# A chain of attention and two mixture-of-experts layers: the descriptor scratch of the software DMA queue at 1024 bytes per partition

## The chip, the cores and the metric

One Trainium2 chip, one core. The metric is the device time of one execution in microseconds (us), as the median of several runs. The engines are TensorE (PE), VectorE (DVE), ScalarE (ACT), GpSimd (POOL) and SyncE (SP). DMAs that SP or ACT issue go through a hardware queue; DMAs that POOL issues go through the software queue, which is the one that the change touches.

## The reference

Three layers in a row, on 4 batches of 576 tokens with 8 heads of 64 (2304 rows of 512).

```python
scores = q @ k.T / 8;  cum = cumsum(max(s, 0))
scores = where(causal, -1e9, scores + min(cum_j - cum_i, 0))
x = softmax(scores) @ v                           # rows of 8*64 = 512
# first mixture: 8 experts, each takes at most 288 rows, best logits first
logits = x @ w_gate;  assigned = greedy(order of all logits, cap = 288)
out[mask_e] = relu(x[mask_e] @ w1[e]) @ w2[e]
# second mixture, of out: only rows with x @ w_skip > 0
e = argmax(xc @ w_gate2);  p = softmax(xc @ w_gate2)[e]
y[mask_e] = xc + p * (relu(xc @ v1[e]) @ v2[e])   # other rows keep x
```

## The kernel before

Attention runs head by head in a hand-written order of steps. Heads come in 16 groups of two; for 15 of them POOL loads keys and queries a second time with a DMA that rounds them to the matmul's 32-bit form (`load_a`, L88; the first of these groups as two half loads, so 16 such DMAs). The rows of attention's output and the logits go to a scratch tensor `xs` in HBM through SP.

The first mixture routes expert by expert: VectorE and TensorE find the 288 rows of an expert by counting, and put their numbers in `tok`. For each expert, POOL gathers the rows in three indirect DMAs of 96 (`gather`, L993), TensorE multiplies them through both weight matrices, and POOL scatters the three results to `out` (`outp`, L1093). For the last expert the gathered rows are first scattered once as they are (`claim`, L1105), so that their places are taken. Each scatter is followed by a memset of one element, the spacer.

The second mixture sorts the rows that are computed into lists of 128 for each expert (`tab`, `tk`), with the number of lists in `nt`. It gathers 128 rows with an indirect DMA (`gather2`, L1241), skips list places that hold no row, multiplies, and scatters the results (`ffn2`, L1333; `ffn2s` for up to 64 rows, L1395). The order of instructions within an expert comes from a planner (`Plan`) with estimated durations; each engine then runs its own queue in that order, held by semaphores.

After the first list of an expert, a register that holds the number of its lists decides whether more is to be done:

```python
        rn = nc.values_load(nt[0:1, e:e + 1], min_val=0, max_val=NJ)      # L1510
        ...
            with tc.If(rn == 2):                                          # L1516
                ffn2s(e, i2, col(tk, e, 1), tabp[:, 1, e, 1:2])
            ...
            with tc.If(rn > 2):                                           # L1520
                ffn2(e, i2, 2, col(tk, e, 1), tabp[:, 1, e, 1:2])
...
    with tc.If(rm > 3):                                                   # L1560
```

L1560 is the case of an expert with more than three lists, behind the last expert. Every engine loads the number and branches for itself. Each branch holds a scatter; where it is skipped, POOL runs an INC_SWDGE_SEM in its place, so that the software queue's semaphores stand as if the scatter had run. The kernel ends (L1622) with SP reading all semaphores, a DRAIN on each engine and a barrier.

[...]

## Time and profile before

| | |
|---|---|
| median of 3 runs | 731.12 us (728.97 to 734.17) |
| profiled execution | 729.32 us; span from the first to the last instruction 727.5 us |
| granted TensorE clock, mean | 0.967 |
| TensorE busy | 660.5 us, 91% of the span |
| VectorE, ScalarE, GpSimd busy | 73%, 55%, 37% |
| software queue (q0) | 7008 packets, 24.25 MB, 12.6% of the DMA engines' time |
| hardware queue of SP (q1) | 28272 packets, 94.87 MB, 41.3% |

Times within the profile count from the first instruction. "Busy" leaves out the queues' own instructions: branches, register loads, semaphores, drains and the issuing of DMAs. The view of one source line lists them too, with an engine's name followed by q.

### The profile page before, as it was taken

Reading aid. Unit: us, or ns where it says so; the run is one execution under the profiler, and the core shown is the slowest. Engines: PE = TensorE matmul, PEld = TensorE weight load, DVE = VectorE, ACT = ScalarE, POOL = GpSimd, SP = SyncE. Lnnn points to the kernel's source line nnn. Section 1 sums busy time; section 2 is a strip of 40 time slices with the busy share of each in tenths; the row PEclk is TensorE's granted clock in tenths of the full one; section 3 lists DMA queues with packets and bytes.
Section 4 is the critical chain, followed back from the end, with each engine's and each line's share of the span. In section 5 each row is a group of like instructions: output and inputs, shape, how many; then the busy total and the mean of one; then the engine's idle time right before and its main releaser. Section 6 shows DMA issues by size and latency. Waiting matters only on the chain. (4 is left out here: it accounts for less than half of the span.)

```text
span 727.5 us, 14103 instructions
## 1 busy us (share of the span) xinstructions
PE 660.5 (91%) x4666; PEld 575.3 (79%) x4667; DVE 531.1 (73%) x1604; ACT 403.3 (55%) x910; POOL 269.3 (37%) x379
## 2 busy tenths in 40 slices
PE   4689999999996489999999999999999999999990
PEld 4578989989895368888988898999987878777770
DVE  7568888798886687888989898644486195884640
ACT  8758888888883132442524334443372274884540
POOL 4799769968720410302212232430204032321200
PEclk9989999999998589999999999999999999999996
DMA  7867897897612343562716346740395076695400
GB/s 161 186 160 184 193 233 163 204 207 170 173 37 74 116 153 116 175 243 60 279 55 247 139 164 240 247 148 1 108 405 208 14 272 246 243 332 207 133 9 14
DMA packets 35939, 122.25 MB, mean 168 GB/s; under 512 B 6480, under 2 KB 6480, under 8 KB 34064
## 3 DMA queue, kind: packets, MB, share of 16 engines
q1 hardware_dynamic: 28272, 94.87, 41.3%
q0 software_dynamic: 7008, 24.25, 12.6%
q10 hardware_dynamic: 576, 2.10, 0.9%
q8 instruction: 43, 0.70, 0.4%
q14 instruction: 40, 0.33, 0.1%
HBM read 101.12 MB, written 13.76 MB: 158 GB/s over the span
## 5 line engine op out<-in xcount | busy, mean ns | idle before, releaser
L987 DVE TENSOR_TENSOR wl<-raw,wh 128x1024 fp32r<-128x1024 f32 x112 | 134.3, 1216 | 22.7 <-ACT wh L985 21.5
L985 ACT CAST wh<-raw 128x1024 fp32r<-128x1024 f32 x112 | 115.0, 1048 | 36.2 <-DMA raw<-in_w_dram 23.7
L256 ACT ACTIVATE z<-z,sums 128x576 f32<-128x576 f32 (+2 forms) x144 | 84.7, 589 | 3.4 <-DVE sums L248 1.7
L248 DVE CUSTOM_DVE_ANT_0 z<-s,mask 128x576 f32<-128x576 f32 (+2 forms) x144 | 70.3, 513 | 14.5 <-PE s L237 14.0
L272 PE MATMUL pt<-ident,z 128*128 128x128 f32 (+1 forms) x464 | 77.4, 282 | 1.6 <-DVE ptl L291 1.2
L236 PE MATMUL s<-kq 128*128 128x288 f32 (+2 forms) x192 | 63.7, 343 | 11.8 <-ACT kq L114 8.8
L291 DVE TENSOR_TENSOR ptl<-pt,pth 128x512 fp32r<-128x512 f32 (+2 forms) x128 | 68.1, 551 | 7.4 <-ACT pth L286 7.1
L993 POOL DMA_INDIRECT xb<-xs,k_tok x24 | 29.6, 1234 | 113.3 <-DVE k_tok L739 34.4
L1049 PE MATMUL y<-hf,rb 128*128 128x288 f32 x256 | 70.5, 411 | 0.0
L1093 POOL DMA_INDIRECT out_dram<-xb,k_tok x24 | 27.0, 1126 | 110.9 <-ACT xb L1076 99.8
L286 ACT CAST pth<-pt 128x512 fp32r<-128x512 f32 (+2 forms) x128 | 59.3, 474 | 12.7 <-PE pt L272 10.0
L237 PE MATMUL s<-ka,qa 128*128 128x288 f32 (+2 forms) x192 | 52.3, 309 | 6.8 <-DMA qa<-kq 3.8
L272 PEld LDWEIGHTS pt<-ident,z 128*128 128x128 f32 (+1 forms) x464 | 52.8, 142 | 6.7 <-issue 2.8
L1051 ACT CAST yr<-y 128x288 fp32r<-128x288 f32 x32 | 12.8, 399 | 72.7 <-PE y L1049 69.4
L1049 PEld LDWEIGHTS y<-hf,rb 128*128 128x128 f32 x256 | 45.5, 189 | 9.0
L300 PE MATMUL y<-pth,vhl 128*128 128x384 f32 (+2 forms) x160 | 50.5, 324 | 0.2 <-ACT yT L317 0.2
L1018 PE MATMUL h<-xth,wh 128*128 128x288 f32 x256 | 48.6, 308 | 1.4 <-DVE r_ac L663 0.9
L236 PEld LDWEIGHTS s<-kq 128*128 128x128 f32 x192 | 37.0, 193 | 15.6 <-issue 13.6
L1018 PE MATMUL h<-xth,wl 128*128 128x288 f32 x256 | 46.6, 299 | 0.0
L1018 PE MATMUL h<-xtl,wh 128*128 128x288 f32 x256 | 46.4, 300 | 0.1
L300 PE MATMUL y<-ptl,vhl 128*128 128x384 f32 (+2 forms) x160 | 46.1, 317 | 0.0
L143 POOL TENSOR_TENSOR qa<-raw,kq 64x576 fp32r<-64x576 f32 x30 | 42.6, 1419 | 5.5 <-DMA kq<-in_kqT_dram 3.6
(343 smaller groups left out, 1729.7 us busy)
## 6 DMA issues: line engine op xcount, KB each, us to landing
raw<-in_v_dram SPq DMA_DIRECT2D x64, 512.0 KB
raw<-in_w_dram SPq DMA_DIRECT2D x46, 512.0 KB
raw<-in_kqT_dram SPq DMA_DIRECT2D x14, 576.0 KB
kq<-in_kqT_dram POOLq DMA_DIRECT2D x14, 576.0 KB, 7.2
rb<-in_w_dram SPq DMA_DIRECT2D x14, 512.0 KB
vraw<-in_vL_dram SPq DMA_DIRECT2D x16, 320.0 KB
xs<-xb SPq DMA_DIRECT2D x16, 288.0 KB
ka<-kq SPq DMA_DIRECT2D x14, 288.0 KB
```

What stands on the lines that cost most here:

```text
L236: nc.tensor.matmul(rows[:, o + c0:o + c1], qs_, kb[:, i, c0:c1], start=True, stop=False)
L237: nc.tensor.matmul(rows[:, o + c0:o + c1], ql_, ka[:, i, c0:c1], start=False, stop=True)
L248: nc.vector.tensor_tensor_reduce(z[:, :w], ps[:, o:o + w], mk, op0=OP.add, op1=OP.min, scale=-0.125, scalar=3e38, accum_out=sums[h // 2][: ...
L256: nc.scalar.activation(z[:, :w], z[:, :w], AF.Exp, bias=sm[:, 0:1], scale=-1.0, accum_out=sm[:, 1:2])
L272: nc.tensor.transpose(ps[:jw, k, :], p[:, I0[jb]:I0[jb] + jw], ident)
L286: nc.scalar.copy(hview(PTB[h % 2][0], ib, jbs), ps[:, :len(jbs), :])
L291: nc.vector.tensor_tensor(hview(PTB[h % 2][1], ib, jbs), ps[:, :len(jbs), :], hview(PTB[h % 2][0], ib, jbs).bitcast(F32), op=OP.subtract)
L300: nc.tensor.matmul(y[:, a2 - 192:S - 192], vhl[:, h % G, jb].rearrange("p a d -> p (a d)"), PTB[h % 2][t][:, jb, a2 - 192:], start=n_ == 0 ...
L985: return nc.scalar.copy(WH[j], RAW[i])
L987: op("DVE", 1.13, f"raw{i} wh{j}a wh{j}b", v, lambda: V.tensor_tensor(WL[j], RAW[i], WH[j].bitcast(F32), op=OP.subtract), pr)
L1018: x = nc.tensor.matmul(ps, a[(p * HC + k) % NP][:, m * 128:(m + 1) * 128], xt[c][:, k, :], start=k == 0 and i == 0, stop=k == 3 and i == 2)
L1049: op("PE", 0.49, f"rb{r} hf{k}", f"yb{b}", lambda r=r, o=o, k=k: nc.tensor.matmul(ps, RB[r][:, o:o + 128], hf[:, k - HS1, :], start=False, ...
```

## The change

The program is built with a descriptor scratch of 1024 bytes per partition. The tiles then begin 15360 bytes lower in each partition; their sizes and order are as before, and so is every instruction on every engine.

```diff
@@ -1612,7 +1612,7 @@
 
     data = dict(**host_layout(q, k, v, s, moe_w_gate),
                 **host_moe(moe_w1, moe_w2, moe2_w_gate, moe2_w_skip, moe2_w1, moe2_w2))
-    nc = bacc.Bacc("TRN2", target_bir_lowering=False, num_devices=1)
+    nc = bacc.Bacc("TRN2", target_bir_lowering=False, num_devices=1, dynamic_dma_scratch_size=1024)
     arrays, args = {}, []
     for name in _INS:
         a = np.ascontiguousarray(data[name])
```

## Rows read from the trace of the kernel before

**Rows 1.** Busy us by stretch; columns: stretch, length, PE, PEld, DVE, ACT, POOL, clock, DMA.

```profile
560.00:711.00 151.00, 144.04 (x703) 116.21 (x702) 93.99 (x105) 86.21 (x117) 31.05 (x48) 1.00 0.51 179
711.00:727.50 16.50, 0.00 (x0) 0.00 (x0) 0.00 (x0) 0.00 (x0) 0.00 (x0) 0.58 0.04 15
```

**Rows 2.** Instructions in order of time, all engines, 708 to 728 us; start, length.

```profile
709.80 0.99 POOL L1333 DMA_INDIRECT out_dram<-xb,tk  x1 [10.54 <-DVEq L1516]
710.77 0.09 POOL L1335 MEMSET spacer<- 1x1 f32 x1
```

**Rows 3.** Single source lines: count, ns min/median/max, first and last start (some in windows).

```profile
L1615 POOLq INC_SWDGE_SEM  x1: 31/31/31, 0.2 to 0.2; - x1
...
L1516 POOLq INC_SWDGE_SEM  x5: 1780/1920/2080, 597.5 to 711.0; - x5
...
L1520 POOLq INC_SWDGE_SEM  x6: 1726/1894/2075, 599.6 to 713.4; - x6
...
L1516 POOLq INC_SWDGE_SEM  x1: 1780/1780/1780, 597.5 to 597.5; - x1
...
L1520 POOLq INC_SWDGE_SEM  x1: 1726/1726/1726, 599.6 to 599.6; - x1
...
L1516 POOLq INC_SWDGE_SEM  x1: 2080/2080/2080, 711.0 to 711.0; - x1
...
L1520 POOLq INC_SWDGE_SEM  x1: 2075/2075/2075, 713.4 to 713.4; - x1
...
L1560 POOLq INC_SWDGE_SEM  x1: 2099/2099/2099, 716.6 to 716.6; - x1
```

**Rows 4.** Single source lines: the kernel's start (L1615) and end (L1622).

```profile
L1615 POOLq DRAIN  x1: 196/196/196, 0.4 to 0.4; - x1
...
L1622 SPq EVENT_SEMAPHORE  x14: 17/28/28, 718.6 to 727.5; - x14
...
L1622 POOLq DRAIN  x3: 46/103/7992, 718.7 to 727.2; - x3
L1622 SPq DRAIN  x3: 7/7/13, 719.4 to 726.9; - x3
```

**Rows 5.** DMA issues of POOL, whole span: count, KB each, median us to landing.

```profile
kq<-in_kqT_dram POOLq DMA_DIRECT2D x14, 576.0 KB, 7.2
...
kq<-in_kqT_dram POOLq DMA_DIRECT2D x2, 288.0 KB, 7.0
...
out_dram<-xb,k_tok POOLq DMA_INDIRECT x27, 4.1
xb<-xs,k_tok POOLq DMA_INDIRECT x24, 3.9
...
xb<-out_dram,tk POOLq DMA_INDIRECT x15, 5.8
out_dram<-xb,tk POOLq DMA_INDIRECT x11, 4.6
...
xb<-out_dram,tks POOLq DMA_INDIRECT x2, 7.1
out_dram<-xb,tks POOLq DMA_INDIRECT x2, 3.8
```

**Rows 6.** DMA issues of POOL, 598 to 728 us.

```profile
xb<-out_dram,tk POOLq DMA_INDIRECT x9, 5.9
out_dram<-xb,tk POOLq DMA_INDIRECT x9, 4.0
```

**Rows 7.** POOL in order of time, 546 to 561 us; five DMAs between these two.

```profile
546.48 0.94 POOL L1093 DMA_INDIRECT out_dram<-xb,k_tok  x1 [0.44 <-ACT xb L1076]
...
559.88 1.03 POOL L1333 DMA_INDIRECT out_dram<-xb,tks  x1 [0.23 <-issue]
```

**Rows 8.** Waits of TensorE: us in total, times, longest.

```profile
PE tr L1004 <- DMA xb<-xs,k_tok: 1.8, 2, 1.5
```

**Rows 9.** DMA issues of POOL, 709 to 728 us.

```profile
out_dram<-xb,tk POOLq DMA_INDIRECT x1, 3.5
```

## The prediction

> **What bounds the kernel now.** I read the busy time by stretch first [rows 1]. From 560 to 711 us TensorE is busy for 144.04 of 151 us: there the matmuls set the pace, and what GpSimd (POOL) does beside them is cover. The last 16.5 us are different in kind: no engine has a busy microsecond in them. The list of instructions in order of time [rows 2] says the same: the last counted instruction is the spacer memset behind the last scatter, which ends at 710.86, and the span ends at 727.5. The chain of waits stops there as well, because it follows counted work only. So the question for this change is what fills 16.6 us in which nothing computes.

> The view of single source lines answers it, since it also lists the queue's own instructions, which are not counted as busy. For each `tc.If` whose branch is skipped, POOL runs one INC_SWDGE_SEM, which books the scatter that the branch would have issued: five on L1516, six on L1520, one on L1560 [rows 3]. The last three start at 711.0, 713.4 and 716.6 and take 2.080, 2.075 and 2.099 us, one behind the other. Then POOL's DRAIN of the kernel's end (L1622) starts at 718.7 and takes 7.992 us [rows 4]. The sum is 6.25 + 7.99 = 14.2 us; loads, branches and the closing barrier are the rest. The program's end waits for POOL's queue alone.

> **The change, part by part.** It adds and moves no instruction; it cuts the room to a sixteenth.

> How many entries n stay listed: if 97 fit in 16384 bytes, at least 97 / 16 = 6 fit in 1024; above that the trace sets no bound but 97. I take 6, the proportion that the rows give, and keep both ends below.

> INC_SWDGE_SEM at the end: 0.30 + 6 x 0.0184 = 0.41 in place of 2.085, three times: 5.03 us less. With the price of the empty queue, 0.031, it would be 6.2.

> DRAIN: 6 x 0.082 = 0.49 us in place of 7.99. What is late next is SyncE, which reads its semaphores from 718.6 and reaches its own drain at 719.4 [rows 4], 0.8 us behind the third INC_SWDGE_SEM. So 8.0 us shrink to 0.8, not to 0.5: 7.2 less. The last scatter doesn't stand in the way: issued at 709.80, it lands 3.5 us later [rows 9], at 713.3, and the new drain would begin at 718.7 - 5.0 = 713.7. That margin is only 0.4 us, so a late landing would be the next bound.

> The nine earlier INC_SWDGE_SEM shrink by about 1.5 us each, 13 us of POOL's queue. I count them at nothing: they lie in 597 to 711, where TensorE is nearly full [rows 1]. If that cover is gone, the gathers behind them only start earlier.

> Taking old entries off is new work, 97 - 6 = 91 times. The nearest row is the DRAIN's 0.082 per entry: 7.5 us over the whole of POOL, which has room. It is on the path of the end where TensorE waits for a gather today, the first three gathers [rows 8], and at the last scatter: 4 x 0.082 = 0.33 us more. Bounds: nothing at all (the entry landed long ago), or 0.30 each, the intercept above: 1.2.

> Waiting for room is the wait that the change may add. Behind a gather that waits stand POOL's next gathers and scatters, and TensorE's transposes wait for the rows. The closest packing that the traced order shows is the DMA at 559.88; with room for six, the one that it must push out was issued at 546.48, 13.4 us earlier [rows 7], and the slowest kind lands in 7.2 [rows 5]. So if the oldest goes first, nobody waits.

> All tiles move 15360 bytes down. No row shows a cost that depends on an address; I take zero.

> Sum: -5.03 - 7.2 + 0.33 = -11.9 us. The profiled execution took 729.32 us with a span of 727.5, so it becomes 717.4. It lies 1.8 under the median of the three runs, 731.12; against that median the forecast is 719.2.

> Each further entry in the list costs 3 x 0.0184, and 0.082 once the drain passes SyncE's 0.8. With 20 entries the gain is 10.3; with 48, half of today's, 6.4. The best case (0.031 for INC_SWDGE_SEM, no cost of taking off) gains 13.4.

> [...]

> **The rivals.**
> *The end's drain is a fixed cost.* If the 7.99 us wait for something other than the list (say, all earlier writes), only the three INC_SWDGE_SEM shrink: -5.03 + 0.33 = -4.7, or 726.4. For it: there is one long DRAIN only, so its slope is not measured, as that of INC_SWDGE_SEM is. Against it: the last DMA landed 5 us before it began, and it fits 97 equal steps. [...]

> *The list isn't bounded by the scratch.* If the bookkeeping lives elsewhere and is only cleared by the last drain, no step changes, and the time is 731.1. For it: nothing in the trace shows an entry being dropped. Against it: a room that is reused has to know which of its users are done.

> *Room is freed by waiting for the newest, not the oldest.* Then POOL stops each time the room is full until all that it holds has landed: 97 / 6 = 16 stops of about 4.9 us (the medians of rows 5 weighted by their counts). It decides from the point at which more than two of them are on TensorE's path, since two cost 9.8 and the end gives back 11.9. With four, 731.1 - 11.9 + 19.6 = 738.8, slower; with eight, 758. For it: gathers come in groups of two to five, and TensorE has waited for one already [rows 8]. [...]

> **How the numbers follow.** Forecast 0.77, fixed drain 0.06, unbounded list 0.10, waiting for the newest 0.07. The likeliest gives 719.2. Its own range: best case 717.7 less 2.2 for the lowest of the runs shown, so 715.5; worst case with 20 entries and 1.2 for taking off, gain 9.4, so 721.7, plus 3 for the highest run. To hold 8 in 10 it has to take in the fixed drain: 715 to 727.5. A measurement of this kernel tells about 1% from no change (the three runs span 0.7%): faster by that means under 723.8, which is the forecast but for its edge, 0.75; within 1% are the fixed drain, the unbounded list and that edge, 0.18; slower is the last rival, 0.07.

> **What would show each step.** POOL's INC_SWDGE_SEM on L1516, L1520 and L1560 near 0.4 us and no longer growing; the long DRAIN on L1622 under 1 us; the stretch behind the last scatter about 5 us in place of 16.6; everything up to 711 us in place within its noise. I am wrong if INC_SWDGE_SEM still grows past 1 us, if the DRAIN stays near 8 while INC_SWDGE_SEM falls, or if POOL's indirect DMAs take several us each or TensorE's waits for gathers exceed the 1.8 us of now [rows 8].

## The result

The change made the kernel faster, by a little over half of what was forecast. The changed kernel's median is 724.83 us (722.98 to 727.07, four runs) against 731.49 us for the kernel before on the same chip; the ratio is 0.9906, with a 95% interval of 0.9881 to 0.9932. That is 6.7 us less, where 11.9 were forecast, and short of the 1% from which the prediction would have called it faster (under 723.8). The interval and the repeats below show that it is no chance. The profiled execution took 724.78 us with a span of 723.1.

The end did what the prediction said. The time ahead of the end did not stay in place: it grew by about 6 us. The experiments are about where these come from.

### The profile page after: what moved, and what is told of

Its sections match the earlier page's. It is cut to its first block, busy times and chain, and to the rows that moved or that the text cites. A ratio compares the mean times of both kernels' runs of the same rounds, so it can differ in the third digit from the quotient of the medians.

```text
span 723.1 us, 14104 instructions
## 1 busy us (share of the span) xinstructions
PE 667.0 (92%) x4667; PEld 581.1 (80%) x4667; DVE 531.7 (74%) x1604; ACT 402.3 (56%) x910; POOL 269.2 (37%) x379
## 5 line engine op out<-in xcount | busy, mean ns | idle before, releaser
L987 DVE TENSOR_TENSOR wl<-raw,wh 128x1024 fp32r<-128x1024 f32 x112 | 134.4, 1216 | 23.0 <-ACT wh L985 19.7
L1018 PE MATMUL h<-xth,wh 128*128 128x288 f32 x256 | 50.5, 318 | 2.0 <-DVE r_ac L663 0.9
L1018 PE MATMUL h<-xtl,wh 128*128 128x288 f32 x256 | 48.4, 309 | 0.1
L1018 PE MATMUL h<-xth,wl 128*128 128x288 f32 x256 | 48.1, 306 | 0.0
L236 PEld LDWEIGHTS s<-kq 128*128 128x128 f32 x192 | 37.0, 193 | 13.4 <-issue 11.1
```

The lines of the kernel that those rows point to most:

```text
L236: nc.tensor.matmul(rows[:, o + c0:o + c1], qs_, kb[:, i, c0:c1], start=True, stop=False)
L987: op("DVE", 1.13, f"raw{i} wh{j}a wh{j}b", v, lambda: V.tensor_tensor(WL[j], RAW[i], WH[j].bitcast(F32), op=OP.subtract), pr)
L1018: x = nc.tensor.matmul(ps, a[(p * HC + k) % NP][:, m * 128:(m + 1) * 128], xt[c][:, k, :], start=k == 0 and i == 0, stop=k == 3 and i == 2)
```

## The profile after

**The end.** Instructions in order of time, all engines, from 716 us; they answer to [rows 2]:

```profile
717.96 0.99 POOL L1333 DMA_INDIRECT out_dram<-xb,tk  x1 [10.55 <-DVEq L1516]
718.94 0.09 POOL L1335 MEMSET spacer<- 1x1 f32 x1
```

Busy us by stretch of the changed kernel, to [rows 1]:

```profile
560.00:719.00 159.00, 152.29 (x739) 122.63 (x737) 99.44 (x123) 86.62 (x118) 36.09 (x56) 1.00 0.49 176
719.00:723.10 4.10, 0.00 (x0) 0.00 (x0) 0.00 (x0) 0.00 (x0) 0.03 (x1) 0.53 0.18 59
```

Single source lines of the changed kernel, to [rows 3, 4]:

```profile
L1516 POOLq INC_SWDGE_SEM  x5: 240/280/340, 605.9 to 719.2; - x5
...
L1520 POOLq INC_SWDGE_SEM  x6: 252/270/286, 606.6 to 719.8; - x6
...
L1560 POOLq INC_SWDGE_SEM  x1: 299/299/299, 721.1 to 721.1; - x1
...
L1622 POOLq DRAIN  x3: 46/103/642, 721.5 to 722.8; - x3
L1622 SPq DRAIN  x3: 7/7/13, 722.2 to 722.5; - x3
```

INC_SWDGE_SEM takes 0.24 to 0.34 us throughout and no longer grows; the long DRAIN is 0.642 us in place of 7.992. Behind the last spacer lie 4.1 us in place of 16.6, so the end gave 12.5 us; the prediction had 12.2.

**The loss.** The last scatter starts at 717.96, not at 709.80 [rows 2]. So 8.2 us of this profile were lost before it. Following instruction by instruction, the changed kernel is 1.4 us ahead of the kernel before when the first list of tokens is ready, and 4.6 us behind when the second expert's first gather starts (296.51 against 291.94; before, then after):

```profile
291.94 1.17 POOL L993 DMA_INDIRECT xb<-xs,k_tok  x1 [34.39 <-DVE k_tok L739]
```

```profile
296.51 1.18 POOL L993 DMA_INDIRECT xb<-xs,k_tok  x1 [38.05 <-DVE k_tok L739]
```

The place is the first expert's start. First the kernel before, GpSimd (POOL) and VectorE (DVE) in order of time:

```profile
252.60 0.16 DVE L739 SCALAR_TENSOR_TENSOR k_tok<-r_iv 96x3 int32<-96x3 f32 x1
...
253.66 1.07 POOL L993 DMA_INDIRECT xb<-xs,k_tok  x1 [8.69 <-DVE r_v L605]
...
253.82 1.22 DVE L987 TENSOR_TENSOR wl<-raw,wh 128x1024 fp32r<-128x1024 f32 x1
...
255.03 0.93 POOL L993 DMA_INDIRECT xb<-xs,k_tok  x1 [0.30 <-issue]
255.41 1.34 DVE L622 TENSOR_TENSOR r_ge<-r_kb,th 128x1134 bf16<-128x1134 f32 x1 [0.38 <-PE y L1410]
...
256.27 1.28 POOL L993 DMA_INDIRECT xb<-xs,k_tok  x1 [0.30 <-issue]
```

Then the same instructions of the changed kernel:

```profile
251.25 0.16 DVE L739 SCALAR_TENSOR_TENSOR k_tok<-r_iv 96x3 int32<-96x3 f32 x1
...
252.46 1.22 DVE L987 TENSOR_TENSOR wl<-raw,wh 128x1024 fp32r<-128x1024 f32 x1
252.53 2.10 POOL L993 DMA_INDIRECT xb<-xs,k_tok  x1 [8.93 <-DVE r_lo L629]
...
254.06 1.34 DVE L622 TENSOR_TENSOR r_ge<-r_kb,th 128x1134 bf16<-128x1134 f32 x1 [0.37 <-PE y L1410]
...
254.93 1.26 POOL L993 DMA_INDIRECT xb<-xs,k_tok  x1 [0.30 <-issue]
255.31 2.35 DVE L987 TENSOR_TENSOR wl<-raw,wh 128x1024 fp32r<-128x1024 f32 x2
...
256.50 1.96 POOL L993 DMA_INDIRECT xb<-xs,k_tok  x1 [0.30 <-issue]
```

Read the order first. Before, the first gather starts 0.90 us after the list of tokens (252.76 to 253.66) and 0.16 us ahead of VectorE's subtraction. After, it starts 1.12 us behind the list (251.41 to 252.53), and the subtraction has begun 0.07 us earlier. Now the ends: the subtraction ends at 253.68 and the gather at 254.63, 0.95 us behind; the comparison on L622 ends at 255.40 and the second gather at 256.19, 0.79 behind; the pair on L987 ends at 257.66 and the third at 258.46, 0.80 behind. Each of these gathers seems to wait for the VectorE instruction that was running when it started, and the third gather of the kernel before does so too (255.41 + 1.34 = 256.75, end at 257.55). From the list to the end of the third gather it was 4.79 us and is 7.05, 2.26 more. (The list of tokens is written on L739; its end is counted.)

What follows on TensorE, in order of time: the last transposes of the first expert and its first matmuls, in the kernel before,

```profile
262.61 0.52 PE L1004 MATMUL tr<-ident,xb 96*128 96x96 f32 x4 [1.53 <-DMA xb<-xs,k_tok]
...
263.70 1.05 PE L1018 MATMUL h<-xth,wh 128*128 128x288 f32 x6 [0.46 <-ACT xth L1008]
```

and in the changed kernel:

```profile
264.46 0.87 PE L1004 MATMUL tr<-ident,xb 96*128 96x96 f32 x4 [2.77 <-DMA xb<-xs,k_tok]
...
265.91 1.81 PE L1018 MATMUL h<-xth,wh 128*128 128x288 f32 x6 [0.45 <-ACT xth L1008]
```

The waits of TensorE say the same, to [rows 8]:

```profile
PE tr L1004 <- DMA xb<-xs,k_tok: 4.7, 3, 2.8
```

The same six matmuls take 1.81 us for 1.05. Busy time and granted clock from 262 to 270 us show why, before and after:

```profile
262.00:270.00 8.00, 6.92 (x63) 6.35 (x64) 6.02 (x15) 3.34 (x6) 0.00 (x0) 1.00 0.36 144
```

```profile
262.00:270.00 8.00, 5.08 (x30) 4.51 (x30) 3.17 (x9) 2.37 (x3) 0.00 (x0) 0.50 0.30 97
```

Behind the longer wait the granted clock stays at 0.50 through this stretch, where it was 1.00. TensorE gets 30 matmuls done instead of 63.

From the list of tokens to the second expert's first gather it is 39.18 us before and 45.10 after. The other profiles place the loss there too: 45.21 and 44.83 us in the next two at 1024 bytes, 37.8 to 40.3 in every profile below in which the first gather came before VectorE's instruction and none waits for room.

## Experiments

Three causes were open: the tiles that moved 15360 bytes down, the small queue itself, and chance in one execution. "Default" is the scratch of the kernel before, 16384 bytes: the 1024 of the change and the 15360 by which it moved the tiles. In the table, "ahead" is the median less what the profile has behind the start of the last scatter; for the kernel before it is 712.0 to 712.6 in the first three comparisons and 710.5 in the last. "Lead" is how long the first gather starts ahead of VectorE's large instruction (below zero: behind its start); that is the subtraction on L987, and in the run with POOL held back more the comparison on L622.

| kernel | lead, us | first three gathers, us | clock 262 to 270 | last scatter | median us | ahead | ratio to before |
|---|---|---|---|---|---|---|---|
| before | +0.16 | 1.07, 0.93, 1.28 | 1.00 | 709.80 | 731.49 | 712.0 | 1 |
| changed (1024) | -0.07 | 2.10, 1.26, 1.96 | 0.50 | 717.96 | 724.83 | 718.0 | 0.9906 (0.9881 to 0.9932) |
| changed, again | -0.06 | 2.10, 1.27, 1.96 | 0.50 | 715.64 | 724.06 | 717.3 | 0.9893 (0.9871 to 0.9916) |
| 1024, tiles not moved | -0.07 | 2.10, 1.26, 1.96 | 0.50 | 717.87 | 724.52 | 717.5 | 0.9899 (0.9878 to 0.9921) |
| 8192, tiles not moved | +0.16 | 1.07, 0.93, 1.28 | 1.00 | 708.69 | 720.57 | 710.5 | 0.9855 (0.9826 to 0.9883) |
| 8192 | +0.15 | 1.07, 0.93, 1.28 | 1.00 | 710.85 | 722.87 | 712.9 | 0.9880 (0.9852 to 0.9908) |
| 2048 | +0.17 | 1.08, 0.93, 1.28 | 1.00 | 709.44 | 719.70 | 712.1 | 0.9848 (0.9817 to 0.9880) |
| default, POOL held back | +0.15 | 1.08, 0.93, 1.25 | 0.79 | 713.51 | 731.71 | 712.2 | 0.9997 (0.9977 to 1.0017) |
| 1024, VectorE held back | +0.38 | 1.07, 1.02, 0.96 | 0.79 | 713.85 | 720.31 | 713.5 | 0.9842 (0.9817 to 0.9867) |
| 512 | +0.01 | 1.07, 0.94, 1.12 | 0.89 | 710.67 | 718.05 | 711.2 | 0.9820 (0.9789 to 0.9851) |
| default, POOL held back more | -0.19 | 2.08, 1.85, 0.92 | 0.59 | 722.75 | 738.44 | 719.0 | 1.0103 (1.0077 to 1.0128) |
| 256 | 0.00 | 1.08, 0.93, 1.15 | 0.67 | 734.27 | 740.39 | 733.7 | 1.0144 (1.0115 to 1.0174) |

**The changed kernel again**, with no edit.

> The changed kernel once more, on the chip of the next three runs, to see how much of the 8.2 us that the profile of after lost ahead of the last scatter comes back. Theory that the loss belongs to the change (by the ring or by the addresses): the last scatter starts at 717 to 720 us, as against 709.80 in the profile of before, and the median is 0.988 to 0.993 of before. Theory that it was the chance of that one execution: the last scatter starts near 711 us and the median is 0.983 to 0.985 of before. Either way the tail is the same: the three INC_SWDGE_SEM of the end take 0.25 to 0.35 us each, the DRAIN of POOL 0.64 us, and 4.1 us lie between the end of the last spacer and the end of the span.

The loss is the change's: the median is as the first theory has it (0.9893), the last scatter at 715.64 somewhat earlier than it expected, the gathers as before to 0.01 us, the clock at 0.50. In the profile of the changed kernel 2.3 us of the 8.2 are something else; see the last section.

**1024 with the tiles where they were.**

```diff
+        keep.tile([128, 3840], F32, name="pad")
```

> A scratch of 1024 bytes, and an unused tile of 15360 bytes per partition ahead of the tiles of the mixture, so that they lie at the addresses of before. Theory of the addresses (tiles that lie 15360 bytes lower cost the time ahead of the last scatter): the last scatter is back near 711 us, the tail stays at 4.1 us, and the median is 0.983 to 0.985 of before. Theory of the ring (the short list costs the time, by what the queue does at each gather, the first ones above all): the last scatter stays at 717 to 720 us and the median at 0.988 to 0.993, the same as with the tiles moved.

All tiles but four small ones of constants lie where they were, and the loss stays (ahead 717.5, ratio 0.9899). The theory of the addresses falls, and the prediction's zero for them stands.

**8192, with and without the tiles moved.**

```diff
-    nc = bacc.Bacc("TRN2", target_bir_lowering=False, num_devices=1)
+    nc = bacc.Bacc("TRN2", target_bir_lowering=False, num_devices=1, dynamic_dma_scratch_size=8192)
```

and for the first of the two

```diff
+        keep.tile([128, 2048], F32, name="pad")
```

> A scratch of 8192 bytes, half of that of before, with an unused tile of 8192 bytes, so that the tiles lie at the addresses of before. If the room of the scratch sets how many DMAs stay listed, in proportion, about half of the 97 do by the end (48, more if the DMAs take less than a 16th of 16384 bytes each, up to 75): INC_SWDGE_SEM of the end takes 1.2 to 1.7 us by 0.30 + 0.0184 per entry, the DRAIN of POOL 3.9 to 6.2 us by 0.082 per entry, and the tail is 9 to 13 us. If only the scratch of 1024 bytes is special, they are 2.1 and 8.0 us as before. Ahead of the last scatter: theory of the addresses, nothing is lost (last scatter near 711 us); theory of the ring, nothing either, since this list is not yet full at the first gathers at 250 us; so that median 0.991 to 0.996 of before by both, and this run is the partner of the next.

> A scratch of 8192 bytes without the unused tile: the tiles lie 8192 bytes lower than before. Tail as in the run with the unused tile. Theory of the addresses: a shift of 8192 bytes may cost as the one of 15360 did, the last scatter at 714 to 720 us and the median 0.998 to 1.004 of before. Theory of the ring: the last scatter stays near 711 us and the median at 0.991 to 0.996, the same as with the unused tile.

Nothing is lost ahead of the last scatter in either (710.5 and 712.9 against 712.6); the 2.3 us between their medians are within the intervals. INC_SWDGE_SEM of the end takes 0.740, 0.735 and 0.759 us and the DRAIN 2.521: less than expected. Both medians lie under those of 1024 bytes on the same chip (724.06 and 724.52), the one with the tiles moved by 1.2 us only, which the intervals don't tell apart. Single source lines, 8192 with the tiles not moved:

```profile
L1516 POOLq INC_SWDGE_SEM  x5: 440/580/740, 596.4 to 709.9; - x5
...
L1520 POOLq INC_SWDGE_SEM  x6: 386/554/735, 597.2 to 710.9; - x6
...
L1560 POOLq INC_SWDGE_SEM  x1: 759/759/759, 712.8 to 712.8; - x1
```

They still grow, by 0.349 us from the first to the last on L1520 over 18 DMAs (0.0194 each), as before, from a lower start. So DMAs came off this list earlier, many at a time, and it is filling again. By 0.02 us per entry for INC_SWDGE_SEM (2.099 at 97) and 0.082 for the DRAIN (7.992 at 97), about 30 DMAs are listed at the end, an estimate. Where the others came off can be seen. The 75th DMA in order of issue, a scatter on L1333, starts 1.30 us behind the VectorE instruction that writes its data (570.05 to 571.35), and in the other profile with 8192 bytes the same scatter does (1.30); before it is 0.29. Of the ten scatters on L1333 that start 0.28 to 0.29 us behind their data in the kernel before, no other is late at 8192. At 1024 eight of the ten start 0.51 to 0.55 us behind, the same eight in all three profiles. 8192 with the tiles not moved, the kernel before, the changed kernel:

```profile
569.30 0.75 DVE L1329 SCALAR_TENSOR_TENSOR xb<-y,q_er,xb 128x512 f32<-128x512 f32 x1 [1.45 <-PE y L1320]
571.35 1.01 POOL L1333 DMA_INDIRECT out_dram<-xb,tks  x1 [10.98 <-issue]
```

```profile
570.35 0.75 DVE L1329 SCALAR_TENSOR_TENSOR xb<-y,q_er,xb 128x512 f32<-128x512 f32 x1 [1.47 <-PE y L1320]
571.39 1.01 POOL L1333 DMA_INDIRECT out_dram<-xb,tks  x1 [10.39 <-DVE xb L1329]
```

```profile
578.50 0.75 DVE L1329 SCALAR_TENSOR_TENSOR xb<-y,q_er,xb 128x512 f32<-128x512 f32 x1 [1.47 <-PE y L1320]
579.77 1.01 POOL L1333 DMA_INDIRECT out_dram<-xb,tks  x1 [10.86 <-DVE xb L1329]
```

**2048.** The same one-line edit with 2048. The theory by then, that of the collision: at 1024 the first gather starts 1.12 us behind the list of tokens and not 0.90, so 0.07 us behind the start of VectorE's subtraction and not 0.16 ahead of it, and the three gathers then take 2.10, 1.26 and 1.96 us for 1.07, 0.93 and 1.28.

> A scratch of 2048 bytes. [...] With 2048 bytes there should be room for the first gather without taking off (18 DMAs come before it at most, with 8192 bytes 67 stayed listed): gathers of 1.07, 0.93 and 1.28 us, clock 1.00 from 262 to 270, last scatter at 708 to 711 us, INC_SWDGE_SEM of the end 0.2 to 0.55 us, DRAIN 0.5 to 1.6 us, tail 4.0 to 5.3 us, median 0.979 to 0.985 of before. Rival, that any short list costs time in the middle: last scatter at 714 us or later and 0.987 to 0.993.

The theory that any short list costs time in the middle falls. Instructions in order of time, and two single source lines:

```profile
252.72 1.08 POOL L993 DMA_INDIRECT xb<-xs,k_tok  x1 [8.70 <-DVE r_v L605]
...
252.89 1.22 DVE L987 TENSOR_TENSOR wl<-raw,wh 128x1024 fp32r<-128x1024 f32 x1
```

```profile
L1560 POOLq INC_SWDGE_SEM  x1: 419/419/419, 712.9 to 712.9; - x1
...
L1622 POOLq DRAIN  x3: 46/103/1132, 713.3 to 715.0; - x3
```

The gather starts 0.89 us behind the list of tokens (251.83), as with the default scratch, and so ahead of VectorE. The ratio is 0.9848.

**Default scratch, POOL held back.** Ahead of the first gather on POOL:

```diff
+            if p == 0 and k == 0:
+                nc.gpsimd.tensor_copy(slack, tok[:, 0:3])
+                nc.gpsimd.tensor_scalar(slack, slack, 1.0, None, op0=OP.add)
```

> The default scratch, and on GpSimd two instructions on 96x3 numbers of a tile of their own between the wait for the list of tokens and the first gather, which hold that gather back by 0.3 to 0.5 us, so that VectorE's subtraction begins first. Theory of the collision: the first three gathers take about 1.8 to 2.1, 1.2 and 1.9 us, the clock stays at 0.50 for some of 262 to 270 us, the last scatter starts at 713 to 718 us, and the median is 1.004 to 1.012 of before, though nothing of the queue is changed. Theory that the short list itself makes these gathers slow: they keep 1.07, 0.93 and 1.28 us and come 0.3 to 0.5 us later, and the median is 0.998 to 1.003.

A miss: the gather still started 0.15 us ahead of VectorE (253.43 and 253.58), so the collision was never made, and the time is that of before.

**1024, VectorE held back.** Ahead of VectorE's subtraction, in the first conversion of weights only:

```diff
+            if n == 0:
+                V.memset(slack, 0.0)
+                for _ in range(2):
+                    V.tensor_scalar(slack, slack, 1.0, None, op0=OP.add)
+            return V.tensor_tensor(WL[j], RAW[i], WH[j].bitcast(F32), op=OP.subtract)
```

> A scratch of 1024 bytes, and on VectorE a memset and two additions on 128x18 numbers of a tile of their own right ahead of the subtraction that the first gather ran into, which hold it back by about 0.4 us. Theory of the collision: the first gather still starts 1.07 us behind the end of its wait, but ahead of the subtraction, and takes 1.07 us, the next two 0.93 and 1.3; the clock is 1.00 from 262 to 270 us, the last scatter starts at 708 to 712 us, the tail stays at 4.1 us, and the median is 0.979 to 0.985 of before. Theory that the short list itself makes these gathers slow: 2.10, 1.26 and 1.96 us as in the changed kernel, last scatter at 715 to 719, median 0.988 to 0.993.

(That text counts from the end of the gather's wait; from the end of L739 its 1.07 us are 1.12.) In order of time:

```profile
252.94 0.16 DVE L739 SCALAR_TENSOR_TENSOR k_tok<-r_iv 96x3 int32<-96x3 f32 x1
...
254.22 1.07 POOL L1000 DMA_INDIRECT xb<-xs,k_tok  x1 [8.92 <-DVE r_hi L606]
...
254.60 1.22 DVE L994 TENSOR_TENSOR wl<-raw,wh 128x1024 fp32r<-128x1024 f32 x1
...
255.60 1.02 POOL L1000 DMA_INDIRECT xb<-xs,k_tok  x1 [0.30 <-issue]
```

The gather still starts 1.12 us behind the list (253.10 to 254.22), but ahead of the subtraction, and takes 1.07. Three small instructions on VectorE give back 4 us of the loss. The last scatter is 1.9 us later than expected; the clock from 262 to 270 us was 0.79 here, not 1.00.

**512.** The same one-line edit with 512.

> A scratch of 512 bytes, half of the changed kernel's, to see whether the queue then waits for room. If the list is taken off in proportion, 2 to 4 DMAs stay listed: INC_SWDGE_SEM of the end 0.18 to 0.26 us, DRAIN 0.25 to 0.45 us, tail 3.7 to 4.0 us. If no DMA has to wait for an older one's transfer, the middle is as in the changed kernel (0.986 to 0.993 of before) or, if the first gather needs no taking off here, as in the run with 2048 bytes (0.978 to 0.985). If room is waited for, gathers that follow each other on POOL at 0.31 us in the changed kernel start 1 to 5 us apart from the third or fourth on, the transfers of the first mixture come late, and the median is 0.995 or more.

The first three gathers follow each other at 0.30 us. INC_SWDGE_SEM of the end is down to 0.219 and the DRAIN to 0.492 us, a little over what was expected, and the median is the lowest of all, 718.05. The lead is 0.01 us only:

```profile
251.96 1.07 POOL L993 DMA_INDIRECT xb<-xs,k_tok  x1 [8.86 <-DVE r_lo L629]
251.97 1.25 DVE L987 TENSOR_TENSOR wl<-raw,wh 128x1024 fp32r<-128x1024 f32 x1
```

The gather goes through, and VectorE's instruction takes 0.03 us longer. One later gather does come late, 1.07 us behind the one ahead of it, where every other profile but that of 256 bytes has about 0.30 at the same place. It may wait for room; no row says so:

```profile
421.93 2.04 POOL L993 DMA_INDIRECT xb<-xs,k_tok  x1 [1.07 <-PE rt L643]
```

**Default scratch, POOL held back more.** Three more of the additions on POOL.

> The run before with GpSimd held back did not test what it should: the gather still started 0.15 us ahead of VectorE's subtraction, because part of the 0.85 us between the wait and the gather went on meanwhile. Here three more additions on 96x3 numbers stand on GpSimd ahead of the first gather, with the default scratch; it should start 0.3 to 0.9 us after the subtraction has begun. Theory of the collision: the gather ends about 0.95 us behind the end of the subtraction, the next two run into VectorE's next instructions in the same way (1.2 to 1.4 and 1.6 to 2.0 us for 0.93 and 1.28), TensorE's granted clock is 0.50 for most of 262 to 270 us, the last scatter starts at 715 to 720 us, the tail is that of before, and the median is 1.004 to 1.012 of before. Theory that it takes the short list: gathers of 1.07, 0.93 and 1.28 us that come 0.6 to 1 us later, and 0.998 to 1.003 of before.

(The 0.85 us of that text, too, count from the end of the gather's wait; from the end of L739 they are 0.90.) POOL and VectorE in order of time:

```profile
254.26 2.33 POOL L998 TENSOR_SCALAR slack<-slack 96x3 f32<-96x3 f32 x4
...
254.99 1.22 DVE L988 TENSOR_TENSOR wl<-raw,wh 128x1024 fp32r<-128x1024 f32 x1
...
256.58 1.34 DVE L622 TENSOR_TENSOR r_ge<-r_kb,th 128x1134 bf16<-128x1134 f32 x1 [0.37 <-PE y L1417]
256.77 2.08 POOL L999 DMA_INDIRECT xb<-xs,k_tok  x1 [0.18 <-issue]
...
259.16 1.85 POOL L999 DMA_INDIRECT xb<-xs,k_tok  x1 [0.30 <-issue]
```

One of the additions took 1.23 us, where the median of the four is 0.32, while VectorE's subtraction ran; so the gathers came later than planned, and the first ran into L622: it ends at 258.85, 0.93 us behind the end of L622 (257.92). With nothing of the queue changed, the first gather takes 2.08 us and the kernel loses 8.4 us. The direct delay is part of that: from the list of tokens (253.92) to the end of the third gather (262.23) it is 8.31 us, 3.5 more than in the kernel before. It shows that the slow gather needs no short list, and what a late first gather costs; it is no measure of the collision alone.

**256.** The same one-line edit with 256.

> A scratch of 256 bytes, a quarter of the changed kernel's: by the proportion of listed DMAs to bytes (30 at 8192, 7 at 1024, 3 at 512) one or two DMAs have room. Theory that room is then waited for: a gather that follows another on POOL at 0.31 us in the kernel before starts only when an earlier transfer has landed, 1 to 3 us later, so that bursts of three are 2 to 6 us longer; INC_SWDGE_SEM of the end 0.17 to 0.21 us and the DRAIN 0.3 to 0.5 us; with 8 mixtures whose gathers come well ahead of their use and a first one that is waited for, the last scatter starts at 712 to 725 us and the median is 0.984 to 1.003 of before. Theory that ended DMAs are taken off without waiting at any length: gathers at 0.31 us, last scatter at 709 to 713 us, and 0.978 to 0.985.

(The eight mixtures of that text are the experts of the first mixture.) Here room is waited for. POOL in order of time:

```profile
254.61 1.08 POOL L993 DMA_INDIRECT xb<-xs,k_tok  x1 [8.86 <-DVE r_lo L629]
255.99 0.93 POOL L993 DMA_INDIRECT xb<-xs,k_tok  x1 [0.30 <-issue]
258.33 1.15 POOL L993 DMA_INDIRECT xb<-xs,k_tok  x1 [1.41 <-DMA xb<-xs,k_tok]
```

Two gathers go out at 0.30 us, the third waits 1.41 us until an earlier transfer has landed. It is the first one's, which lands 3.2 us after its issue, at 257.81; the second one's lands at 259.19, when the third gather has long begun (258.33). INC_SWDGE_SEM is down at 0.186 and the DRAIN at 0.208 us. The loss is larger than expected: the last scatter starts at 734.27, not by 725, and the kernel is slower than before by 1.4%.

## Why the prediction was right at the end and short in the middle

*The number.* 724.83 us lies in the stated range of 715 to 727.5, but by luck: the range was widened to take in a drain that doesn't shrink, and what filled it was a loss in the middle. The forecast's own worst case ended at 724.7. Two of the prediction's own signs were against it: TensorE's waits for gathers rose from 1.8 to 4.7 us, and the kernel up to the last scatter did not stay in place.

*The list.* Right. INC_SWDGE_SEM on L1560 and the long DRAIN are 2.099 and 7.992 us at 16384 bytes, 0.759 and 2.521 at 8192, 0.419 and 1.132 at 2048, 0.299 and 0.642 at 1024. Between neighbours the one falls 4.1 times as far as the other each time (5.471 / 1.340, 1.389 / 0.340, 0.490 / 0.120), as if both walk the same list. Below 1024 they part: 0.219 and 0.492 at 512, 0.186 and 0.208 at 256. At 512 the DRAIN ends about when the last scatter lands (issued at 710.67, 3.6 us to landing), so it may have waited for that. With 97 at 16384 and one price per entry they give about 30, 13 and 7 entries at 8192, 2048 and 1024, estimates. The prediction's 6 for 1024 was close, though not by proportion: 8192 held 30 at the end and not 48, since most of the list seems to have come off together at the 75th DMA. The intercept of 0.30 us was too high (the changed kernel's median on L1516 is 0.28, with a few listed), and the 0.031 of the best case too low: in no run does an INC_SWDGE_SEM on these lines take under 0.162. The DRAIN was 0.64, not 0.49, still about as long as what SyncE does meanwhile. The rivals of the fixed drain and of the unbounded list are out.

*The end.* Forecast -12.2, measured -12.5.

*The earlier INC_SWDGE_SEM counted at nothing.* Right. From the first of them to the last scatter the kernel before takes 112.3 us (597.5 to 709.8) and the changed one 112.1 (605.9 to 717.96), though POOL spends some 14 us less in them.

*Tiles moved: zero.* Right, by the run with the unused tile.

*Waiting for room: none.* Right at 1024, where the gaps between the gathers of a burst are those of before. At 512 one gather may wait, at 256 gathers wait, and 23 us are lost ahead of the last scatter (733.7 against 710.5). That is the loss the rival had, but not its mechanism: the one wait that the rows above resolve was for the oldest of the gathers and not for the newest.

*Taking old entries off: the term that failed.* The prediction said that the first three gathers are on TensorE's path and gave them 0.082 us each, 0.33 in all with the last scatter, 1.2 at most. The delay is more than 0.082 and within the bound: the first gather starts 0.22 us later behind its list at 1024, 0.15 to 0.16 at 512 and 256, and not at all at 2048 and 8192, where by the estimates the list was not yet full. But it cost 4.7 to 6.0 us ahead of the last scatter (717.3 and 717.5 against 712.6, 718.0 against 712.0). The prediction priced a delay by its own length. At this place the order of two events mattered: 0.22 us put the gather behind the start of a VectorE instruction that it had beaten by 0.16. The chain that the runs show is 0.22 us at the queue, 2.26 us at the third gather, then a longer TensorE wait (2.77 us for 1.53), then matmuls at a granted clock of 0.50 for 1.00, 5.9 us in all by the second expert's first gather, counted from the list of tokens. Holding VectorE back by 0.4 us at 1024 takes the collision away, and holding POOL back at 16384 makes it. That the 0.22 us is the taking off itself is inferred from the sizes at which it appears and from the scatters, which are late by as much at 1024 and, once, by 1.0 us at 8192; no row names it. How the loss behind the gathers divides between the wait and the clock wasn't tested apart.

What ties the gather to VectorE was not shown; the times were. The VectorE instructions are a subtraction of 1.22 us and a comparison of 1.34. Of the first expert's gathers in all the profiles, those that start behind the start of one of them end 0.79 to 0.95 us behind its end, and the others take 0.92 to 1.08 us. But a gather that starts first doesn't hold VectorE for its length: the subtraction takes 1.22 us, begun 0.16 us behind the gather, and 1.25 begun 0.01 behind it. Which part of a gather is held no row tells.

Without the collision the forecast of 11.9 us holds nearly to the number: 1024 bytes with VectorE held back gains 11.5 us, 2048 gains 12.1 and 512 gains 13.8, each against the kernel before on its chip. The intervals at 512 (0.9789 to 0.9851) and with VectorE held back (0.9817 to 0.9867) are clear of the changed kernel's (0.9881 to 0.9932). The run at 512 is 1.8% under before, but by a lead of 0.01 us; at 2048 the lead is 0.17.

## What to carry to other kernels

Instructions that are not counted as busy, INC_SWDGE_SEM and DRAIN, held 14.2 of the last 16.6 us of this kernel; when the profile's last stretch has no busy engine, look them up by their source lines and see whether they grow. A small delay on a path where an engine waits had no fixed price here (0.22 us at the first gather went with 4.7 to 6.0 us ahead of the last scatter): look at what stands on the neighbouring engine within a few tenths of a microsecond, and ask whether the order of the two can flip. With a scratch whose size goes with the length of a list (about 30, 13 and 7 entries at 8192, 2048 and 1024 bytes, estimates), try more than one size: here 512 and 2048 were both better than 1024, and 256 was slower than the default. Most of what lies between 512 and 1024 is on which side of one VectorE instruction one gather fell: with VectorE held back, 1024 has a ratio of 0.9842, against 0.9820 at 512.

## What was not expected

- A gather that starts 0.01 us ahead of VectorE's instruction takes 1.07 us, one that starts 0.07 us behind takes 2.10.
- At 8192 bytes some 67 DMAs seem to have come off the list together, and the scatter that starts late there pays 1.0 us for it, 0.015 us each, an estimate; at 1024 a late start pays 0.22 to 0.27.
- A gather can be held longer than by one instruction. In the kernel before, the first gather of a later expert starts beside VectorE's subtraction, and two more VectorE instructions follow with no gap (to 421.06); it ends 0.83 us behind the last of them:

```profile
418.87 3.02 POOL L993 DMA_INDIRECT xb<-xs,k_tok  x1 [0.35 <-issue]
```

- The granted clock from 410 to 425 us was 0.91 in the profile of the changed kernel and 1.00 in the second profile of the same program. From that later expert's first gather to the next one's first (424.09 to 457.72, and 424.28 to 455.41) the first took 33.6 us and the second 31.1. Profiles with other scratch sizes show either value, the kernel before 1.00. These 2.5 us differ between executions of one program; they are why one profile showed 8.2 us lost where the medians show 5 to 6. What sets them is open.
